# Odd pairs of heads on exchanged halves of the partitions in a retention and feed-forward kernel

## The chip, the cores and the metric

The kernel runs on one core of one Trainium2 chip. The metric is the device time of one execution in microseconds (us), the median of several runs. Engines are named as in the profile: PE is TensorE (PEld its weight loads), DVE is VectorE, ACT is ScalarE, POOL is GpSimd, SP is SyncE, which issues the DMAs (SPq is its queue).

## What is computed

The reference takes q, k and v of 4 batches, 8 heads, 576 positions and 64 values a head, and computes a retention, followed by two feed-forward parts:

```python
scores = scale * np.matmul(q, k.transpose(0, 1, 3, 2))
Dmat = np.where(rel >= 0, gamma[:, None, None] ** rel[None, :, :], 0.0)
ret = scores * Dmat[None, :, :, :]
x = np.matmul(ret, v)            # then (B*S, H*D) = 2304 x 512
a, b = x @ w1, x @ w2            # 512 -> 1024
x = (a * b @ w3) @ w_out         # 1024 -> 1024 -> 512
h = x @ w_in                     # 512 -> 2048
g = np.maximum(h, 0) + alpha * np.minimum(h, 0)
out = g @ w_out                  # 2048 -> 512
```

The change is in the retention alone.

## The kernel before

The retention is computed in chunks of 128 positions (four of 128 and one of 64), with a running state of 64 x 64 per head. Two heads make a pair: head 2p of pair p has its q and k on partitions 0 to 63, head 2p+1 on partitions 64 to 127 (`HEADS`). Four pairs make a batch. All products of the retention are of fp32 operands.

For a chunk c the class `Retention` issues, on PE, in this order within one step (`steps`, L340): `scores(c+1)`, `values(c)`, `moments(c+1)`.

- `scores` (L256) multiplies the keys of a chunk by its queries, for each pair m and each half `pp` of the partitions: 64 rows of the array, 128 columns, into one bank for each half (L274). The last chunk gives 64 x 64 (L264). VectorE multiplies the result by a mask into `rt` (L277; `rte` for the last chunk, L266).
- `moments` (L281) multiplies scaled keys by values: 128 rows, 64 columns of the array, 64 wide (L288). VectorE makes the new state of it (L294, L296, L298), with the decay `gc` of each head.
- `values` (L303) makes the output `o` of a chunk: state times queries (L312: rows `pp`, columns `pp`), then `rt` times v (L320: 128 rows, 64 columns; for the last chunk `rte` times the end of v, rows and columns `pp`). So of the four quarters of the array that a 64 x 64 product can lie in, L312 uses the two on the diagonal. `o` has two buffers of one bank each. VectorE multiplies `o` by `qs` (L327), ScalarE rounds the result to `xh` (L172), VectorE takes the rest as `xl` (L173).

```python
for m, p in enumerate(self.pairs):
    for pp in HEADS:
        nc.tensor.matmul(o[pp, m, 0:w], self.state[c - 1][pp, m], qk[p][pp, 0, i0:i0 + w],
                         start=(m == 0), stop=False, skip_group_check=True)
```

PE, ACT and SP work their instructions in the order in which the program issues them. VectorE's and ScalarE's parts are put into a list (`later`) and issued at the next `flush()`. ScalarE also scales the keys of a batch before its first moments (`prep`, L253).

Batch 0 is computed first, by itself: pairs 0 and 1 (`r0`, `s0`) and pairs 2 and 3 (`r1`, `s1`) are two sequences of steps that are merged by a written-out order (L392), with two pairs in each step. Its loads are issued at the very start by SP: `per_row` (kd and gc, L375), then for each pair qk (L358), kv (L359) and the pair's constants `per_pair` (mask, mtail and qs, L361), with two loads of weights between. Before the first loads land, PE runs 16 products on zeros (L385).

Then the products by w1 and w2 begin (`ab_unit`, `gemm3`, L179), in sets of 12 products of 128 x 512. Batches 1, 2 and 3 are computed with four pairs in a step, and `cycle` (L450) puts their steps between those sets: batch 1 at 7/6 steps a set, so that two steps may follow each other at once (and what is left follows at L472), batch 2 at 7/15, batch 3 at 7/9. The loads of a batch are issued where the one before has freed the tiles: those of batch 1 after the last step of `s0` (L399) and after batch 0 (L406), those of batch 2 at L475, those of batch 3 at L487. A load waits until the load eight before it has landed, as the kernel's program has eight semaphores for loads. After 220 us nothing of the retention is left.

Of the kernel before, what the change touches and what calls it, by code (L numbers as in the profile page):

```python
# [7 lines left out]
F32 = mybir.dt.float32  # L8
# [4 lines left out]
ALU = mybir.AluOpType  # L13
PSUM = bass.MemoryType.PSUM
DRAM = bass.MemoryType.DRAM

P = 128
B, H, S, D = 4, 8, 576, 64
NPAIR = H // 2
NT, DM, DF1, DF2 = B * S, 512, 1024, 2048  # L20
CH = 128
# [4 lines left out]
HEADS = (slice(0, 64), slice(64, 128))  # L26
# [111 lines left out]
def retention_moe_kernel(ctx: ExitStack, tc, qk, kv, w_out1, w3t, w12, w_in, w_out2, alpha, c_row, c_pair, out):  # L138
    nc = tc.nc

    def pool(stack, name, bufs=1, **kw):
        return stack.enter_context(tc.tile_pool(name=name, bufs=bufs, **kw))
# [14 lines left out]
    idle = tmp.tile([P, 512], I32, tag="b", name="idle", bufs=2).bitcast(BF16)  # L157
# [12 lines left out]
    def split(hi, lo, src):  # L170

        nc.scalar.copy(hi, src)  # L172
        nc.vector.tensor_tensor(out=lo, in0=src, in1=_f32(hi), op=ALU.subtract)  # L173
# [51 lines left out]
    per_pair = decay.tile([P, NPAIR, 3 * CH + 64], F32, name="per_pair")  # L225
    mask = per_pair[:, :, 0:2 * CH].rearrange("p n (h i) -> p h n i", h=2)
    mtail = per_pair[:, :, 2 * CH:2 * CH + 64]
    qs = per_pair[:, :, 2 * CH + 64:]
    per_row = decay.tile([P, 128], F32, name="per_row")[:, 0:H + NPAIR]
    kd, gc = per_row[:, 0:H], per_row[:, H:]  # L230
# [3 lines left out]
    def x_block(n):  # L234
        if n not in xt:
            w = BLOCKS[n][1]
            xt[n] = tuple(xp.tile([P, KT, 512], F32R, tag=f"x{m}", name=f"x{m}{n}", bufs=3)[:, :, :w] for m in "hl")
        return xt[n]

    class Retention:  # L240


# [13 lines left out]
        def scores(self, c):  # L256
            b, n = self.b, self.n
            sc = self.psum["sc"].tile([P, 2, 512], F32, tag="sc", name=f"sc{b}_{c}")
            qk, v = qkt[b], kvt[b]
            if c == NCH - 1:  # L260
                rt = self.rt[c] = attn.tile([P, NPAIR, 64], F32, tag="rte", name=f"rte{b}")[:, 0:n]
                for m, p in enumerate(self.pairs):
                    for pp in HEADS:
                        nc.tensor.matmul(sc[pp, 0, m * 64:(m + 1) * 64], qk[p][pp, 1, 512:S], qk[p][pp, 0, 512:S],  # L264
                                         start=True, stop=True, skip_group_check=True)
                later.append(lambda: nc.vector.tensor_tensor(  # L266
                    out=rt, in0=sc[:, 0, 0:64 * n].rearrange("p (n i) -> p n i", n=n), in1=mtail[:, self.ps],
                    op=ALU.mult))
                return
            i0 = c * CH  # L270
            rt = self.rt[c] = attn.tile([P, 2, NPAIR, CH], F32, tag="rt", name=f"rt{b}_{c}", bufs=2)[:, :, 0:n]
            for m, p in enumerate(self.pairs):
                for j, pp in enumerate(HEADS):
                    nc.tensor.matmul(sc[:, j, m * CH:(m + 1) * CH], qk[p][pp, 1, i0:i0 + CH], qk[p][pp, 0, i0:i0 + CH],  # L274
                                     start=True, stop=True, skip_group_check=True)

            later.append(lambda: nc.vector.tensor_tensor(  # L277
                out=rt, in0=sc[:, :, 0:n * CH].rearrange("p h (n i) -> p h n i", n=n), in1=mask[:, :, self.ps],
                op=ALU.mult))

        def moments(self, c):  # L281

            b, n = self.b, self.n
            v = kvt[b]
            st = self.psum["st"].tile([P, NPAIR, D], F32, tag="st", name=f"st{b}_{c}")[:, 0:n]
            for m, p in enumerate(self.pairs):
                for j, pp in enumerate(HEADS):
                    nc.tensor.matmul(st[pp, m], v[p][:, 4 * j + c], v[p][:, 8 + 4 * j + c],  # L288
                                     start=True, stop=True, skip_group_check=True)

            def state():
                new = attn.tile([P, NPAIR, D], F32, tag="S", name=f"S{b}_{c}", bufs=3)[:, 0:n]
                if c == 0:
                    nc.vector.tensor_copy(new, st)  # L294
                else:
                    nc.vector.tensor_tensor(out=new, in0=self.state[c - 1], in1=gc[:, self.ps].unsqueeze(2)  # L296
                                            .to_broadcast([P, n, D]), op=ALU.mult)
                    nc.vector.tensor_tensor(out=new, in0=new, in1=st, op=ALU.add)  # L298
                self.state = {**(self.state or {}), c: new}

            later.append(state)

        def values(self, c):  # L303
            b, n = self.b, self.n
            w = CH if c < NCH - 1 else 64
            i0 = c * CH
            qk, v, rt = qkt[b], kvt[b], self.rt.pop(c)
            o = self.psum["o"].tile([P, NPAIR, CH], F32, tag="o", name=f"o{b}_{c}", bufs=2)
            if c:
                for m, p in enumerate(self.pairs):  # L310
                    for pp in HEADS:
                        nc.tensor.matmul(o[pp, m, 0:w], self.state[c - 1][pp, m], qk[p][pp, 0, i0:i0 + w],  # L312
                                         start=(m == 0), stop=False, skip_group_check=True)
            for m, p in enumerate(self.pairs):
                for j, pp in enumerate(HEADS):
                    if c < NCH - 1:
                        vj, rj = v[p][:, 8 + 4 * j + c], rt[:, j, m]
                    else:
                        vj, rj = v[p][pp, 16], rt[pp, m]
                    nc.tensor.matmul(o[pp, m, 0:w], vj, rj, start=(c == 0 and m == 0), stop=True,  # L320
                                     skip_group_check=True)
            later.append(lambda: self.decayed(c, o, w))

        def decayed(self, c, o, w):

            x = xsp.tile([P, NPAIR, CH], F32, tag="x", name=f"xs{self.b}_{c}")[:, 0:self.n, 0:w]
            nc.vector.tensor_tensor(out=x, in0=o[:, 0:self.n, 0:w], in1=qs[:, self.ps, 0:w], op=ALU.mult)  # L327
            t0 = self.b * S + c * CH
            cuts = [0] + [t - t0 for t, _ in BLOCKS if t0 < t < t0 + w] + [w]

            def parts():
                for lo, up in zip(cuts, cuts[1:]):
                    n = (t0 + lo) // 512
                    at = t0 + lo - BLOCKS[n][0]
                    xh, xl = (m[:, self.ps, at:at + up - lo] for m in x_block(n))
                    split(xh, xl, x[:, :, lo:up])

            later.append(parts)
# [13 lines left out]

    qkt, kvt = {b: {} for b in range(B)}, {b: {} for b in range(B)}

    def load_pair(b, p):
        qkt[b][p] = attn.tile([P, 2, S], F32, tag=f"qk{p}", name=f"qk{b}_{p}")
        kvt[b][p] = attn.tile([P, 17, D], F32, tag=f"kv{p}", name=f"kv{b}_{p}")
        nc.sync.dma_start(out=qkt[b][p], in_=qk[b, p])  # L358
        nc.sync.dma_start(out=kvt[b][p], in_=kv[b, p])  # L359
        if b == 0:  # L360
            nc.sync.dma_start(out=per_pair[:, p], in_=c_pair[:, p])  # L361

    def load_batch(b):
        for p in range(NPAIR):
            load_pair(b, p)

    def attention_psum(stack, twice):
        return {"sc": pool(stack, f"ps_sc{twice}", bufs=twice, space=PSUM, reuse_waits="tile"),
                "st": pool(stack, f"ps_st{twice}", space=PSUM, reuse_waits="tile"),
                "o": pool(stack, f"ps_o{twice}", space=PSUM, reuse_waits="tile")}  # L370


    first = ExitStack()
    psum0 = attention_psum(first, 2)
    nc.sync.dma_start(out=per_row, in_=c_row)  # L375
    load_pair(0, 0)
    ws.load_until(1)
    load_pair(0, 1)
    ws.load_until(2)
    load_pair(0, 2)  # L380
    load_pair(0, 3)
    nc.sync.dma_start(out=al, in_=alpha)
    warm = psum0["o"].tile([P, 512], F32, tag="o", name="warm", bufs=2)
    for _ in range(16):
        nc.tensor.matmul(warm, idle[:, 0:P], idle[:, :512], start=True, stop=True)  # L385
    r0, r1 = Retention(0, [0, 1], psum0), Retention(0, [2, 3], psum0)
    r0.prep([0])
    ws.tick(2)
# [74 lines left out]
    def retention(b):  # L463
        r = Retention(b, list(range(NPAIR)), psum1)
        return Steps([r.prep] + r.steps())

    r = retention(1)
# [20 lines left out]
    r = retention(3)  # L488
# [25 lines left out]
    turn = 0  # L514
# [48 lines left out]
    for k in range(C1):  # L563
        ws.until(n_w12 + 3 * k + 3)
        for i in range(C1):
            if k == 0:
                acc[i] = bank(i, f"pw{i}")
            h, l = w3p[i // 4, k]
# [181 lines left out]
    for b in range(NB):  # L750
        ys = [bank(b % 2 * 4 + o, f"y{b}_{o}")[:, :W] for o in range(KT)]
        for c in range(C1):
            to_load.tick(1)
            for o in range(KT):
                oc = slice(o * P, (o + 1) * P)
                for i, (a, bb) in enumerate(((0, 0), (0, 1), (1, 0))):
                    nc.tensor.matmul(ys[o], wpc[c][a][:, oc], yab[b, c][:, bb], start=(c == 0 and i == 0),  # L757
                                     stop=(c == C1 - 1 and i == 2))
# [211 lines left out]
    for n, (j, b) in enumerate(steps):  # L970
# [8 lines left out]
        h, l = ready.pop(n)  # L979
        for i in range(NM):  # L980
            ic = slice(i * P, (i + 1) * P)
            for m in range(2):
                wh, wl = wbc[2 * j + m]
                for q, (x, y) in enumerate(((h, wh), (h, wl), (l, wh))):
                    nc.tensor.matmul(accs[b][i], x[:, m, ic], y, start=(j == 0 and m == 0 and q == 0),  # L985
                                     stop=(j == C1 - 1 and m == 1 and q == 2))
# [83 lines left out]
```

## Time and profile before

| | us |
|---|---|
| median of 3 runs | 814.14 |
| lowest and highest run | 812.62, 814.38 |
| profiled execution: its own time | 812.48 |
| profiled execution: its span | 810.7 |

The profile is of one execution. Its rows give starts in us from the start of the span; in a timeline the second number is how long it took, in a group of instructions the busy time and the mean of one in ns. [...]

### The profile page before, as it was taken

How to read it: one execution, taken by the hardware profiler on the slowest of the kernel's cores; microseconds unless marked ns; L12 is line 12 of the kernel's file. 1: busy time of each engine (PE TensorE's matmuls, PEld its weight loads, DVE VectorE, ACT ScalarE, POOL GpSimd, SP SyncE). 2: the span in 40 equal slices, each digit the busy share in tenths (PEclk: the TensorE clock that was granted, in tenths of full speed). 3: DMA queues.
4: the chain of work that ended last, by engine and by line, in shares of the span. 5: the costliest groups of instructions: out<-in, count | busy, mean ns of one | idle time of the engine just before them, and what ended most of it. 6: DMA issues, size and time to landing. Idle time of an engine off the chain costs nothing.

```text
span 810.7 us, 12667 instructions
## 1 busy us (share of the span) xinstructions
PE 793.1 (98%) x4768; PEld 699.9 (86%) x4768; DVE 499.6 (62%) x895; ACT 349.7 (43%) x648; POOL 0.2 (0%) x4
## 2 busy tenths in 40 slices
PE   7989999999999999999999999999999999999998
PEld 4768888888888988999999999999997888888886
DVE  4786776325467789979752568677889923222222
ACT  3452562232245566655534455455566622222221
POOL 0000000000000000000000000000000000000000
PEclk8989999999999999999999999999999999999999
DMA  9845821371076658999934935325566735344341
GB/s 348 300 142 200 303 112 78 105 280 79 27 229 181 213 184 300 308 375 402 394 129 151 380 116 186 127 98 186 172 212 223 238 98 175 97 138 137 98 135 40
DMA packets 78845, 155.91 MB, mean 192 GB/s; under 512 B 7872, under 2 KB 55488, under 8 KB 78784
## 3 DMA queue, kind: packets, MB, share of 16 engines
q1 hardware_dynamic: 78784, 155.10, 54.5%
q8 instruction: 37, 0.61, 0.3%
q14 instruction: 24, 0.20, 0.1%
HBM read 103.69 MB, written 51.38 MB: 191 GB/s over the span
## 4 chain that ended last, share of the span: by engine, by line
PE 92%; DMA 3%; ACT 2%; DVE 1%; SPq 1%; issue 0%; ACTq 0%
PE ps L179 24%; PE o L985 23%; PE h L824 21%; PE y L757 12%; PE pw L571 5%; PE o L320 2%; DMA kv<-in_kv_dram 2%; PE sc L274 2%; PE o L312 1%; DMA gr<-gd 1%; PE st L288 1%; DVE xs L327 0%; ACT xh L172 0%; PE sc L264 0%; DVE gl L173 0%
## 5 line engine op out<-in xcount | busy, mean ns | idle before, releaser
L179 PE MATMUL ps<-xh,w 128*128 128x512 f32 (+1 forms) x640 | 187.5, 374 | 1.8 <-ACT w L112 1.7
L985 PE MATMUL o<-wb,gh 128*128 128x512 f32 x576 | 177.6, 389 | 1.2 <-ACT gh L172 1.2
L179 PEld LDWEIGHTS ps<-xh,w 128*128 128x128 f32 x640 | 116.9, 190 | 23.7 <-ACT w L112 1.9
L985 PEld LDWEIGHTS o<-wb,gh 128*128 128x128 f32 x576 | 108.0, 188 | 24.0 <-ACT gh L172 1.7
L179 PE MATMUL ps<-xl,w 128*128 128x512 f32 (+1 forms) x320 | 118.8, 371 | 0.0
L985 PE MATMUL o<-wb,gl 128*128 128x512 f32 x288 | 112.3, 390 | 0.5 <-DVE gl L173 0.5
L173 DVE TENSOR_TENSOR gl<-gr,gh 128x768 fp32r<-128x768 f32 x48 | 45.9, 957 | 100.2 <-ACT gh L172 100.0
L757 PE MATMUL y<-yab,wp 128*128 128x384 f32 x576 | 100.0, 334 | 0.0
L757 PEld LDWEIGHTS y<-yab,wp 128*128 128x128 f32 x576 | 99.9, 188 | 0.1
L172 ACT CAST gh<-gr 128x768 fp32r<-128x768 f32 x48 | 40.2, 839 | 116.2 <-PE o L985 111.3
L179 PEld LDWEIGHTS ps<-xl,w 128*128 128x128 f32 x320 | 60.9, 190 | 10.0 <-DVE xl L173 0.3
L985 PEld LDWEIGHTS o<-wb,gl 128*128 128x128 f32 x288 | 54.0, 188 | 12.4 <-DVE gl L173 1.3
L836 DVE SCALAR_TENSOR_TENSOR g<-m,al,g 128x384 f32<-128x384 f32 x48 | 29.7, 618 | 48.2 <-ACT g L835 47.9
L824 PE MATMUL h<-xT,wv 128*128 128x384 f32 x288 | 54.9, 334 | 1.4 <-DVE g L842 1.4
L824 PE MATMUL h<-xT,wu 128*128 128x384 f32 x288 | 55.0, 335 | 0.3 <-ACT h L849 0.3
L108 DVE CUSTOM_DVE_ANT_0 a<-a,b 128x1024 uint16<-128x1024 uint16 x72 | 49.5, 687 | 3.8 <-DVE a L106 0.5
L824 PEld LDWEIGHTS h<-xT,wv 128*128 128x128 f32 x288 | 50.3, 188 | 1.8 <-DVE g L842 1.8
L824 PEld LDWEIGHTS h<-xT,wu 128*128 128x128 f32 x288 | 50.3, 188 | 0.9 <-ACT h L849 0.6
L433 ACT CAST ab<-f 128x512 fp32r<-128x512 f32 (+1 forms) x40 | 23.1, 576 | 64.2 <-DVE f L437 59.8
L437 DVE TENSOR_TENSOR f<-f,ps 128x512 f32<-128x512 f32 (+1 forms) x40 | 25.3, 632 | 35.3 <-PE ps L179 35.0
L103 DVE TENSOR_SCALAR a<-a 128x512 f32<-128x512 f32 x72 | 30.4, 422 | 22.2 <-ACT a L93 21.9
L571 PE MATMUL pw<-wo,w 128*128 128x512 f32 x192 | 43.7, 389 | 0.0
(82 smaller groups left out, 1012.9 us busy)
## 6 DMA issues: line engine op xcount, KB each, us to landing
gd<-g SPq DMA_DIRECT2D x96, 192.0 KB, 1.9
gr<-gd SPq DMA_DIRECT2D x96, 192.0 KB, 2.5
abd<-ab SPq DMA_DIRECT2D x32, 512.0 KB, 3.7
raw<-in_w_out_dram SPq DMA_DIRECT2D x24, 512.0 KB, 4.0
qk<-in_qk_dram SPq DMA_DIRECT2D x16, 576.0 KB, 7.1
yab<-abd SPq DMA_DIRECT2D x24, 384.0 KB, 8.5
kv<-in_kv_dram SPq DMA_DIRECT2D x16, 544.0 KB, 7.9
raw<-in_w_dram SPq DMA_DIRECT2D x16, 512.0 KB, 7.4
```

The source lines that it names most:

```text
L103: nc.vector.tensor_scalar(out=a, in0=a, scalar1=self.LEAST, scalar2=self.MOST, op0=ALU.max, op1=ALU.min)
L108: nc.vector.tensor_tensor(out=a.bitcast(I32), in0=a.bitcast(I32), in1=b, op=ALU.add)
L172: nc.scalar.copy(hi, src)
L173: nc.vector.tensor_tensor(out=lo, in0=src, in1=_f32(hi), op=ALU.subtract)
L179: nc.tensor.matmul(ps, a, bb, start=(n == 0), stop=(n == last))
L433: nc.scalar.copy(t[:, 0], f)
L437: nc.vector.tensor_tensor(out=f, in0=f, in1=pss[1], op=ALU.mult)
L571: nc.tensor.matmul(acc[i], a[:, ic], bb, start=(k == 0 and n == 0), stop=(k == C1 - 1 and n == 2))
L757: nc.tensor.matmul(ys[o], wpc[c][a][:, oc], yab[b, c][:, bb], start=(c == 0 and i == 0), stop=(c == C1 - 1 and i == 2))
L824: nc.tensor.matmul(ps, a[:, x, ks], b[:, y, k], start=(fresh and n == 0), stop=(n == 5), skip_group_check=True)
L836: nc.vector.scalar_tensor_tensor(out=g, in0=r, scalar=neg[:, c:c + 1], in1=g, op0=ALU.mult, op1=ALU.add)
L985: nc.tensor.matmul(accs[b][i], x[:, m, ic], y, start=(j == 0 and m == 0 and q == 0), stop=(j == C1 - 1 and m == 1 and q == 2))
```

## The change

- A function `places(p)` gives for each of the two heads of pair p: the half of the partitions on which its q, k and state lie, the half on which its output lies, and the number of the former. For even pairs both are the head's own half, as before; for odd pairs q, k and state lie on the other half, and the output stays.
- The scores, moments, state products and the end of v follow it. Both heads' products are issued head by head as before, so in odd pairs the one on partitions 64 to 127 comes first. The output `o` of even pairs and of odd pairs lies in two banks, and successive chunks take turns in different columns of the same two banks (`values_room`), where before each chunk had a bank to itself, one of two. The first product of each bank has `start`.
- L327 reads both banks in one instruction and writes as before.
- The loads of odd pairs are exchanged: qk as two loads of 64 partitions, kv as one load of its first 16 columns of 64 and two half-loads of the end of v; in batch 0 mask as two loads, mtail as two half-loads and qs as one, where each of these pairs had one load of constants. kd and gc, one load before, are four: kd, gc of even pairs, and two halves of gc of odd pairs.

No arithmetic changes. The core of the diff:

```diff
+    def places(p):
+
+        return [(HEADS[(j + p) % 2], HEADS[j], (j + p) % 2) for j in range(2)]
...
-                    for pp in HEADS:
-                        nc.tensor.matmul(sc[pp, 0, m * 64:(m + 1) * 64], qk[p][pp, 1, 512:S], qk[p][pp, 0, 512:S],
+                    for rows, _, _ in places(p):
+                        nc.tensor.matmul(sc[rows, 0, m * 64:(m + 1) * 64], qk[p][rows, 1, 512:S], qk[p][rows, 0, 512:S],
...
-                for j, pp in enumerate(HEADS):
-                    nc.tensor.matmul(sc[:, j, m * CH:(m + 1) * CH], qk[p][pp, 1, i0:i0 + CH], qk[p][pp, 0, i0:i0 + CH],
+                for rows, _, r in places(p):
+                    nc.tensor.matmul(sc[:, r, m * CH:(m + 1) * CH], qk[p][rows, 1, i0:i0 + CH], qk[p][rows, 0, i0:i0 + CH],
...
-                for j, pp in enumerate(HEADS):
-                    nc.tensor.matmul(st[pp, m], v[p][:, 4 * j + c], v[p][:, 8 + 4 * j + c],
+                for j, (rows, _, _) in enumerate(places(p)):
+                    nc.tensor.matmul(st[rows, m], v[p][:, 4 * j + c], v[p][:, 8 + 4 * j + c],
...
-            o = self.psum["o"].tile([P, NPAIR, CH], F32, tag="o", name=f"o{b}_{c}", bufs=2)
+            o = self.psum["o"](n)
             if c:
                 for m, p in enumerate(self.pairs):
-                    for pp in HEADS:
-                        nc.tensor.matmul(o[pp, m, 0:w], self.state[c - 1][pp, m], qk[p][pp, 0, i0:i0 + w],
-                                         start=(m == 0), stop=False, skip_group_check=True)
+                    for rows, pp, _ in places(p):
+                        nc.tensor.matmul(o[pp, p % 2, m // 2, 0:w], self.state[c - 1][rows, m], qk[p][rows, 0, i0:i0 + w],
+                                         start=(m < 2), stop=False, skip_group_check=True)
             for m, p in enumerate(self.pairs):
-                for j, pp in enumerate(HEADS):
+                for j, (rows, pp, r) in enumerate(places(p)):
                     if c < NCH - 1:
-                        vj, rj = v[p][:, 8 + 4 * j + c], rt[:, j, m]
+                        vj, rj = v[p][:, 8 + 4 * j + c], rt[:, r, m]
                     else:
-                        vj, rj = v[p][pp, 16], rt[pp, m]
-                    nc.tensor.matmul(o[pp, m, 0:w], vj, rj, start=(c == 0 and m == 0), stop=True,
+                        vj, rj = v[p][rows, 16], rt[rows, m]
+                    nc.tensor.matmul(o[pp, p % 2, m // 2, 0:w], vj, rj, start=(c == 0 and m < 2), stop=True,
                                      skip_group_check=True)
...
-            nc.vector.tensor_tensor(out=x, in0=o[:, 0:self.n, 0:w], in1=qs[:, self.ps, 0:w], op=ALU.mult)
+            nc.vector.tensor_tensor(out=x.rearrange("p (i r) w -> p i r w", r=2),
+                                    in0=o[:, :, :, 0:w].rearrange("p r i w -> p i r w"),
+                                    in1=qs[:, self.ps, 0:w].rearrange("p (i r) w -> p i r w", r=2), op=ALU.mult)
...
+    def in_places(p, t, src):
+
+        if p % 2 == 0:
+            nc.sync.dma_start(out=t, in_=src)
+        else:
+            for rows, pp, _ in places(p):
+                nc.sync.dma_start(out=t[rows], in_=src[pp])
+
     def load_pair(b, p):
...
-        nc.sync.dma_start(out=qkt[b][p], in_=qk[b, p])
-        nc.sync.dma_start(out=kvt[b][p], in_=kv[b, p])
-        if b == 0:
+        in_places(p, qkt[b][p], qk[b, p])
+        if p % 2:
+            nc.sync.dma_start(out=kvt[b][p][:, 0:16], in_=kv[b, p, :, 0:16])
+            in_places(p, kvt[b][p][:, 16], kv[b, p, :, 16])
+        else:
+            nc.sync.dma_start(out=kvt[b][p], in_=kv[b, p])
+        if b == 0 and p % 2 == 0:
             nc.sync.dma_start(out=per_pair[:, p], in_=c_pair[:, p])
+        elif b == 0:
+            for h in range(2):
+                nc.sync.dma_start(out=per_pair[:, p, h * CH:(h + 1) * CH],
+                                  in_=c_pair[:, p, (1 - h) * CH:(2 - h) * CH])
+            in_places(p, mtail[:, p], c_pair[:, p, 2 * CH:2 * CH + 64])
+            nc.sync.dma_start(out=qs[:, p], in_=c_pair[:, p, 2 * CH + 64:])
...
+    def values_room(stack, twice):
+
+        t = pool(stack, f"ps_o{twice}", space=PSUM, reuse_waits="tile").tile([P, 2, 512], F32, name=f"o{twice}")
+        turn = [0]
+
+        def take(n):
+            at = turn[0] % 512
+            turn[0] += n // 2 * CH
+            return t[:, :, at:at + n // 2 * CH].rearrange("p r (i w) -> p r i w", w=CH)
+
+        return take
...
-    nc.sync.dma_start(out=per_row, in_=c_row)
+    nc.sync.dma_start(out=kd, in_=c_row[:, 0:H])
+    for p in range(2):
+        in_places(p, gc[:, p::2], c_row[:, H + p::2])
...
-    warm = psum0["o"].tile([P, 512], F32, tag="o", name="warm", bufs=2)
-    for _ in range(16):
-        nc.tensor.matmul(warm, idle[:, 0:P], idle[:, :512], start=True, stop=True)
+    warm = psum0["o"](8).rearrange("p r i w -> p r (i w)")
+    for n in range(16):
+        nc.tensor.matmul(warm[:, n % 2], idle[:, 0:P], idle[:, :512], start=True, stop=True)
```

## Rows read from the trace of the kernel before

**Rows 1.** The profile's page: busy us of each engine, its share of the span, instructions.

```profile
PE 793.1 (98%) x4768; PEld 699.9 (86%) x4768; DVE 499.6 (62%) x895; ACT 349.7 (43%) x648; POOL 0.2 (0%) x4
```

**Rows 2.** Chain of waits over the span, longest pieces: start us, us, what.

```profile
4.20 7.35 DMA kv<-in_kv_dram
...
34.14 8.44 DMA kv<-in_kv_dram
45.76 5.02 PE ps L179 x12
...
114.56 1.09 PE sc L274 x16
```

**Rows 3.** Timeline, a step of batch 2: start us, us, engine, line, operation, records.

```profile
131.24 1.09 PE L312 MATMUL o<-qk,S 64*64 64x128 f32 x16
132.26 1.09 PE L320 MATMUL o<-rt,kv 128*64 128x128 f32 x16
...
133.41 0.69 DVE L327 TENSOR_TENSOR xs<-o,per_pair 128x512 f32<-128x512 f32 x1
...
140.55 1.09 PE L312 MATMUL o<-qk,S 64*64 64x128 f32 x16
```

**Rows 4.** PE's timeline in windows 12.13-12.20, 10.68-10.75, 57.53-57.60: records in each.

```profile
12.13 0.27 PE L288 MATMUL st<-kv 128*64 128x64 f32 x1 [1.12 <-ACT kv L253]
...
10.68 0.28 PE L288 MATMUL st<-kv 128*64 128x64 f32 x2
...
57.36 0.44 PE L312 MATMUL o<-qk,S 64*64 64x128 f32 x4
```

**Rows 5.** Timeline, the last two steps of batch 1 (68 to 74 us).

```profile
71.95 0.68 PE L312 MATMUL o<-qk,S 64*64 64x64 f32 x16
72.07 0.69 DVE L327 TENSOR_TENSOR xs<-o,per_pair 128x512 f32<-128x512 f32 x1 [0.46 <-PE o L320]
72.32 0.33 SPq L358 DMA_DIRECT2D qk<-in_qk_dram  x1
...
72.47 0.63 PE L320 MATMUL o<-rte,kv 64*64 64x64 f32 x16
...
73.25 0.50 PE L179 MATMUL ps<-xh,w 128*128 128x512 f32 x1 [0.15 <-ACT xh L172]
```

**Rows 6.** Chain of waits in batch 0, the state products on it.

```profile
16.78 1.05 PE o L312 x8
```

**Rows 7.** Stretches: us, busy by engine (records), PE's clock, DMA share, GB/s.

```profile
7.00:13.00 6.00, 2.16 (x19) 1.34 (x18) 2.93 (x5) 3.03 (x6) 0.00 (x0) 0.96 1.03 419
13.00:19.20 6.20, 6.20 (x56) 5.22 (x56) 5.65 (x14) 2.15 (x4) 0.00 (x0) 0.50 1.03 415
...
28.00:32.40 4.40, 4.00 (x64) 2.94 (x64) 3.48 (x11) 1.11 (x3) 0.00 (x0) 1.00 1.01 407
32.40:34.00 1.60, 1.21 (x13) 0.98 (x12) 1.13 (x5) 0.41 (x1) 0.00 (x0) 1.00 0.74 223
34.00:39.00 5.00, 5.00 (x24) 3.87 (x24) 2.73 (x6) 3.62 (x8) 0.00 (x0) 1.00 0.90 286
```

**Rows 8.** Timeline of SP's queue, issues of loads: start us, us, line.

```profile
0.73 0.39 SPq L375 DMA_DIRECT2D per_row<-const_row_dram  x1
1.17 0.42 SPq L358 DMA_DIRECT2D qk<-in_qk_dram  x1
...
25.62 0.33 SPq L358 DMA_DIRECT2D qk<-in_qk_dram  x1
```

**Rows 9.** Timeline of batch 0: scaling, moments and a tail's neighbours.

```profile
19.70 1.70 ACT L253 ACTIVATE kv<-kv,per_row 128x256 f32<-128x256 f32 x4
...
22.00 0.45 PE L288 MATMUL st<-kv 128*64 128x64 f32 x8
...
25.25 0.45 PE L312 MATMUL o<-qk,S 64*64 64x64 f32 x8
...
25.74 0.41 DVE L327 TENSOR_TENSOR xs<-o,per_pair 128x256 f32<-128x256 f32 x1
```

More of the change, by code (lines that the diff above doesn't have):

```diff
@@ L369, in attention_psum @@
                 "st": pool(stack, f"ps_st{twice}", space=PSUM, reuse_waits="tile"),
-                "o": pool(stack, f"ps_o{twice}", space=PSUM, reuse_waits="tile")}
+                "o": values_room(stack, twice)}
     first = ExitStack()
     psum0 = attention_psum(first, 2)
-    nc.sync.dma_start(out=per_row, in_=c_row)
+    nc.sync.dma_start(out=kd, in_=c_row[:, 0:H])
+    for p in range(2):
+        in_places(p, gc[:, p::2], c_row[:, H + p::2])
     load_pair(0, 0)
```

## The prediction

> **What bounds the kernel now.** I read the busy shares first [rows 1]: TensorE is busy 98% of the span, VectorE 62%, ScalarE 43%, so a gain has to come off TensorE's path, and a new wait anywhere on that path is paid in full. The chain of waits [rows 2] says where this holds. From 45.76 us to the end it is TensorE almost alone. Before that it leaves TensorE twice, both times for a load of keys and values: 7.35 us that land at 11.57 (batch 0, pair 1) and 8.44 us that land at 42.62 (batch 1, pair 3). After the second, ScalarE has to scale the keys before it turns to other work, and TensorE goes on at 45.76. So the change has three stages to be costed: batch 0 (to 33.2 us), the wait for batch 1's loads, and batches 1 to 3 among the large products.
>
> In the last of these, one step of a batch of four pairs is a run of small products [rows 3]: after eight scores (1.09 us, start to start [rows 2]) eight state products take 1.02 (131.24 to 132.26), then come the products with the values. An fp32 product leaves two records, so eight leave 16. I asked how many are under way at once, with very narrow windows [rows 4]. Where only one head's keys were ready (12.13), one record is there in the first 0.07 us; where both heads were ready (10.68), two are. Of the state products, begun at 57.36, four have started by 57.60, two more than the first two: they go in twos, one of each head, and 16 records in 1.02 us make a pair every 0.11 to 0.13, taken as 0.11. Two of the array's corners work, two are idle.
>
> **Part 1: four corners instead of two (gain).** In odd pairs the state and q of a head lie on the other half of the partitions while its output stays, so consecutive pairs use all four corners. If four records go where two went, eight pairs of records become four fours: 4 x 0.11 = 0.44 us off each state group of 1.02. The 64-wide tails (state product and L320 with rte, 0.52 each [rows 5]) go in pairs of about 0.06, so 0.23 off each. Batches 2 and 3 have three wide groups and two tails: 3 x 0.44 + 2 x 0.23 = 1.78 us each, 3.55 together, all on the path, where TensorE is alone [rows 2]. Lower bound 0: no row shows four corners at work.
>
> In batch 1 the tails follow the last wide step at once [rows 5]: L312 begins at 71.95, while VectorE's read of the former output (L327) begins at 72.07 and takes 0.69; the next large product waits for ScalarE, fed by that read. Three wide groups bring 1.31; the tails' gain is hidden by this wait. Moreover both outputs now lie in the same two banks, so I let the tail wait for the read to end, which costs 0.2 more than the gain hides: 1.1 us in all for batch 1. Elsewhere in batches 1 to 3 the read ends long before the next values (134.10 against 140.55 [rows 3]), so sharing the banks costs nothing there. That one half of a bank is guarded against a read of the other is my assumption; below it the price is 0. [...]
>
> In batch 0 a group has two pairs. [...] Two of four pairs fall away each time, the later two at full clock: 0.43 + 0.22 + 0.22 = 0.87. After 23.9 us the chain goes through VectorE and ScalarE, so later savings there count as 0.
>
> **Part 2: order of the other products (0).** Scores and moments of odd pairs now come head 1's half first: A B B A instead of A B A B. Taken one half after the other, each of the three seams in a group of four pairs could cost a slot of 0.11 in scores and 0.06 in moments and tails: 2.2 us a batch, the upper bound. I take 0, the lower: in [rows 4] the second head's first record already starts ahead of the first head's second one, so TensorE passes over work whose corner is busy, and A B B A asks for no more of it.
>
> **Part 3: more and smaller loads (loss).** Issues at the start are 0.44 to 0.47 us apart [rows 8]. kd and gc come as four instead of one: 3 x 0.46 = 1.4 us before the first q and k. Bandwidth is used up from there (419 GB/s and full engines from 7 to 13 us [rows 7]), so everything behind moves by as much.
>
> Pair 1's qk comes as two loads of 64 partitions. The trace has no load of 64 partitions. Whole, its 576 KB take 1.41 us at 419 GB/s. Halved, they take from 1.41 (each half half as long) to 2.82 (each half as long as the whole). I take 2.82: the full stretches move 407 to 419 GB/s whatever they load [rows 7], so I read the limit as one of the path into the partitions, of which a half-load uses half; the lower end would need the other half's path to serve it. Price 1.41 per odd pair. [...]
>
> Pair 1's other added pieces (two for the end of v, two of mask, two of mtail, qs by itself) move the bytes that the whole loads moved. They are issued 0.33 to 0.47 us apart while 1.4 MB is still under way before them, so issuing stays ahead of the transfers: 0 to 0.5, taken as 0, since the queue ran ahead by 7 us before (issue 4.20, landing 11.57). So the landing at 11.57 moves by 1.4 + 1.4 = 2.8. On the way through batch 0: minus 0.87 (part 1). Pair 3's keys come 4.2 later (2.8 and its own 1.41); ScalarE scaled them from 19.70 (behind pair 2's) for moments at 22.00 [rows 9], which TensorE now waits for: 0.6. The first tail of batch 0 (25.25) now waits for a read that begins at 25.74 and takes 0.41 [rows 9]: 0.95. Later reads there are on the VectorE chain already: 0. Shift at the end of pair 0 and 1: 2.8 - 0.87 + 0.6 + 0.95 = 3.5 us. What the lower clock may give back (less work falls into its stretch) or take, I bound by 1.4 either way and take as 0.
>
> Batch 1's eight loads begin there (25.62 [rows 8]) and end at 42.62. Two odd pairs add 2 x 1.41. The dip at 32.4 to 34 (223 GB/s against 407 [rows 7]) came from the second four being issued late, and goes: 0.7; the slower stretch after it (286) may go too: 1.5 more. I take 1.2 back. Shift of the landing, and of 45.76: 3.5 + 2.8 - 1.2 = 5.1 us (from 3.1 to 6.3).
>
> In batches 2 and 3 the added issues and 2.8 us of loading are hidden: batch 2's first load is issued at 72.32 [rows 5], its first product starts at 114.56 [rows 2]. If that cover went, 2.8 would be paid.
>
> **Sum.** -3.55 - 1.1 + 5.1 = +0.45 us against the profiled execution's 812.48 us, which lies 1.7 below the median of the runs, 814.14. Forecast: **814.6 us**, no change that can be told (0.2%, 1.6 us, is about what a measurement of this kernel can tell).
>
> **Rivals.**
> - **Halves cost nothing extra** (1.41 per odd pair falls away). For it: all engines serve either load with packets of the same length. Against it: the reading above. Shift in batch 0: 1.4 - 0.87 + 0.95 = 1.5, without added loading and with 0.9 back: 0.6. Sum -3.55 - 1.1 + 0.6 = -4.0: 810.1 us.
> - **Still two at a time** (slower than before). Place: L312 and L320's tails on TensorE. If the next corner's record starts only when the first corner's second one has, part 1 falls away: 3.55 + 1.1 + 0.87 = 5.5 dearer, 820.1 us; it decides once less than four fifths of that gain comes (1.2 us missing make 815.8, slower by 0.2%). For it: no row has more than two under way. Against it: rows and columns of the array both overlap already [rows 3, 4]. [...]
> - **A B B A stalls**: 2.2 us a batch over three batches, 6.6, to 821.2 us; evidence as in part 2.
> - **The wait for shared banks isn't there**: 0.2 + 0.95 less, 813.5 us; no sign changes.
>
> **How the numbers follow.** Forecast with its bounds 0.60 (814.6, within 811.5 to 817.5); halves for nothing 0.17; two at a time, wholly or in part, 0.18; A B B A 0.05. The range reaches from the first rival's time to near the second's: **810 to 819.5**. Faster by over 0.2%: 0.14 from the first rival and 0.13 from the forecast's lower bounds, 0.27. Slower: 0.21 of the two slower rivals and 0.15 from the forecast's upper bounds, 0.36. Same: 0.37.
>
> **What would show it.** Four records of L312 under way in a window of 0.05 us and groups of 0.6 us instead of 1.02 confirm part 1; groups of 1.02 refute it. Scores still at 1.09 confirm part 2. The landing of batch 0's pair 1 near 14.4 us confirms part 3, near 13 the first rival; TensorE resuming near 50.9 confirms the shift. Idle time of L312 ended by L327 shows the shared banks. If the time from that point to the end is not 4 to 5 us shorter, part 1 is wrong.

## The result and the profile after

The changed kernel took 819.59 us (median of 4 runs, 818.74 to 821.27) beside 813.40 for the kernel before in the same job: ratio 1.0079, 95% interval 1.0061 to 1.0096. That is 6.2 us slower, where no change was forecast, and just outside the range given. The profiled execution took 818.74 us, with a span of 817.0; it is compared below with that of before (812.48 and 810.7), a difference of 6.3.

The busy time of TensorE fell by 3.5 us while the span grew by 6.3, so TensorE waits more. The page of after, against [rows 1]:

```profile
PE 789.6 (97%) x4768; PEld 695.6 (85%) x4768; DVE 498.9 (61%) x895; ACT 349.6 (43%) x648; POOL 0.2 (0%) x4
```

The chain of waits of after (start us, us, what) is to be read against [rows 2]:

```profile
18.30 8.65 DMA kv<-in_kv_dram
26.98 0.92 ACT kv L260 x2
27.89 2.48 issue
...
45.33 6.24 DMA kv<-in_kv_dram
51.57 2.22 issue
...
56.89 5.20 PE ps L179 x12
62.09 1.09 PE sc L281 x16
...
68.71 0.60 PE o L319 x16
...
81.98 0.70 DVE xs L334
82.73 0.46 PE o L319 x16
83.42 41.08 PE ps L179 x180
124.50 1.09 PE sc L281 x16
...
166.20 27.43 PE ps L179 x120
193.63 1.09 PE sc L281 x16
...
224.46 69.50 PE ps L179 x396
```

Before, batch 0's last load on the chain was pair 1's, landing at 11.57. Now it is pair 3's, landing at 26.95, and TensorE resumes among the large products at 56.89 instead of 45.76; this point is called the resumption below. The "issue" at 51.57 is still loading: the keys and values of batch 1's pair 3, issued at 45.33, land 8.4 us later by the load's own record, at 53.72. From the resumption on TensorE is almost alone, as before, and gains. The chain of before has these pieces beside those of [rows 2]:

```profile
50.79 1.09 PE sc L274 x16
...
73.25 41.31 PE ps L179 x180
...
158.09 27.43 PE ps L179 x120
185.52 1.09 PE sc L274 x16
...
218.17 69.50 PE ps L179 x396
```

Cut at these pieces, the two executions and the best of the experiments (e1, below) compare so, in us:

| stage | before | after | e1 |
|---|---|---|---|
| start to the resumption | 45.76 | 56.89 | 44.86 |
| to batch 1's second scores | 5.03 | 5.20 | 5.38 |
| batch 1, to the large products alone | 22.46 | 21.33 | 21.37 |
| to batch 2 | 41.31 | 41.08 | 41.09 |
| batch 2 | 43.53 | 41.70 | 41.70 |
| to batch 3 | 27.43 | 27.43 | 27.43 |
| batch 3 | 32.65 | 30.83 | 30.83 |
| to the end of the span | 592.53 | 592.54 | 592.34 |

Two things happened, and they can be told apart at the resumption: 11.1 us are lost before it, 4.8 are won behind it.

**The gain.** A group of eight state products takes 0.60 us where it took 1.02 [rows 3]. Narrow windows on TensorE's timeline of after (68.75 to 68.80, 68.80 to 68.90) show why: four records have started 0.16 us after the first (by 68.80), eight after 0.26 (by 68.90), where before four had started after 0.24 [rows 4].

```profile
68.64 0.34 PE L319 MATMUL o<-qk,S 64*64 64x128 f32 x4
...
68.64 0.45 PE L319 MATMUL o<-qk,S 64*64 64x128 f32 x8
```

**The loss.** SP's queue in the timeline of after, against [rows 8]: the last large load of pair 1, then weights and pair 2's q and k, then alpha (8 KB, the factor of the second feed-forward part).

```profile
6.79 0.58 SPq L377 DMA_DIRECT2D kv<-in_kv_dram  x1
...
15.33 0.33 SPq L85 DMA_DIRECT2D raw<-in_w_dram  x1
15.71 0.43 SPq L367 DMA_DIRECT2D qk<-in_qk_dram  x1
...
27.04 0.54 SPq L423 DMA_DIRECT2D al<-in_alpha_dram  x1
```

In the timeline of before, pair 2's q and k stand here:

```profile
5.94 0.44 SPq L358 DMA_DIRECT2D qk<-in_qk_dram  x1
```

They were issued at 5.94 before; now at 15.71, when pair 1's big loads had landed (15.32). By then seven small loads behind pair 1's keys hold seven of the eight places, and nothing of size is under way. The stretches of after show it in the last two columns (DMA share, GB/s), where [rows 7] had full engines at 415 to 419:

```profile
7.00:12.80 5.80, 1.26 (x9) 0.52 (x7) 0.57 (x2) 2.12 (x4) 0.00 (x0) 0.80 1.05 316
12.80:14.20 1.40, 0.77 (x2) 0.48 (x2) 1.22 (x3) 0.00 (x0) 0.00 (x0) 0.50 0.92 244
15.70:18.00 2.30, 2.10 (x14) 1.65 (x16) 1.24 (x3) 0.55 (x2) 0.00 (x0) 0.50 0.68 212
```

There are two different losses in it: up to 14.2 the DMA engines are full, or nearly so, and move little (the halves); from 15.7 to 18 they are a third empty (the held queue). A third stands in VectorE's timeline and what surrounds it, to be read against [rows 9]:

```profile
25.34 0.28 DVE L303 TENSOR_TENSOR S<-S,per_row 128x128 f32<-128x128 f32 x1
26.98 0.91 ACT L260 ACTIVATE kv<-kv,per_row 128x256 f32<-128x256 f32 x2 [1.20 <-DMA kv<-in_kv_dram]
28.98 0.18 DVE L844 TENSOR_SCALAR al<-al 128x16 f32<-128x16 f32 x1 [3.35 <-DMA al<-in_alpha_dram]
...
30.00 0.28 DVE L305 TENSOR_TENSOR S<-S,st 128x128 f32<-128x128 f32 x1
...
30.38 0.46 PE L295 MATMUL st<-kv 128*64 128x64 f32 x8 [3.88 <-issue]
```

Pair 3's keys are scaled at 27.89, but the moments start at 30.38. They write the bank that VectorE's L305 reads at 30.00, and L305 stands in VectorE's order behind a small operation on alpha, whose load SP issued last of all. The view says "issue" because the wait is for several things; the last to end, by these rows, is L305 (at 30.28).

Behind that wait stands a fourth loss, in TensorE's clock. From 26.4 to 30.3 us TensorE works 0.10 us; its granted clock is still 1.00 up to 30.9 and then 0.50 up to 34.3. Before, it was 1.00 from 19.5 to 43.2. The same 48 records, from the moments at 30.38 to the end of the stretch at 34.59, against e1 with whole loads (21.67 to 24.38), columns as in [rows 7]:

```profile
30.38:34.59 4.21, 4.21 (x48) 3.26 (x50) 2.85 (x8) 0.54 (x2) 0.00 (x0) 0.59 1.00 403
```

```profile
21.67:24.38 2.71, 2.71 (x48) 2.18 (x50) 2.06 (x7) 0.55 (x2) 0.00 (x0) 1.00 0.94 378
```

So the lower clock takes 1.5 us here. That it fell because TensorE had waited is not shown.

### The profile page after: what moved, and what is told of

It is laid out like the page before. It is cut to its first block, busy times and chain, and to the rows that moved or that the text cites. A ratio compares the mean times of both kernels' runs of the same rounds, so it can differ in the third digit from the quotient of the medians.

```text
span 817.0 us, 12708 instructions
## 1 busy us (share of the span) xinstructions
PE 789.6 (97%) x4768; PEld 695.6 (85%) x4768; DVE 498.9 (61%) x895; ACT 349.6 (43%) x648; POOL 0.2 (0%) x4
## 4 chain that ended last, share of the span: by engine, by line
PE 90%; DMA 5%; DVE 2%; ACT 1%; SPq 1%; issue 1%; ACTq 0%; DVEq 0%
PE ps L179 24%; PE o L1026 22%; PE h L865 21%; PE y L798 12%; PE pw L612 5%; DMA kv<-in_kv_dram 3%; PE o L327 2%; PE sc L281 2%; DMA qk<-in_qk_dram 1%; PE o L319 1%; PE st L295 1%; DMA gr<-gd 1%; SPq L370 0%; DVE gl L173 0%; DMA x2d<-ys 0%
## 5 line engine op out<-in xcount | busy, mean ns | idle before, releaser
L179 PE MATMUL ps<-xh,w 128*128 128x512 f32 (+1 forms) x640 | 187.6, 375 | 1.7 <-ACT w L112 1.7
L179 PEld LDWEIGHTS ps<-xh,w 128*128 128x128 f32 x640 | 117.2, 190 | 23.3 <-ACT w L112 1.8
L179 PE MATMUL ps<-xl,w 128*128 128x512 f32 (+1 forms) x320 | 118.9, 372 | 0.0
L179 PEld LDWEIGHTS ps<-xl,w 128*128 128x128 f32 x320 | 61.0, 191 | 9.7
L103 DVE TENSOR_SCALAR a<-a 128x512 f32<-128x512 f32 x72 | 30.4, 422 | 25.8 <-ACT a L93 25.5
```

The lines of the kernel that those rows point to most:

```text
L103: nc.vector.tensor_scalar(out=a, in0=a, scalar1=self.LEAST, scalar2=self.MOST, op0=ALU.max, op1=ALU.min)
L179: nc.tensor.matmul(ps, a, bb, start=(n == 0), stop=(n == last))
```

## The experiments

Each is an edit of the changed kernel unless another is named. "Resumes" is the first product of L179 after batch 1's loads, as in the table. A time without an interval or a number of runs is of one execution. Executions of one kernel differ by 3 to 5 us (ten of e12: 812.87 to 816.17, ten of e11: 810.25 to 815.27), so these experiments are read by the landings and the resumption in the trace more than by the time. In e2, e5, e6 and e8, moreover, the part behind the retention takes 594.5 to 595.3 us, where all other executions have 592.2 to 592.9: there the granted clock fell to 0.50 once more, between 619 and 640 us. Their times are some 2 us longer in that part, far behind the loads at the start; that the lower clock makes this difference was not tried.

**e1: every load whole.** The order of the halves is put into the layout of the inputs and constants, which the program makes before the launch in any case.

```diff
-            for rows, pp, _ in places(p):
-                nc.sync.dma_start(out=t[rows], in_=src[pp])
...
+        nc.sync.dma_start(out=qkt[b][p], in_=qk[b, p])
+        nc.sync.dma_start(out=kvt[b][p], in_=kv[b, p])
+        if b == 0:
+            nc.sync.dma_start(out=per_pair[:, p], in_=c_pair[:, p])
```

> The changed kernel with the inputs and constants of odd pairs laid out in exchanged halves beforehand, so that every load is whole, as many and as large as in the kernel before; products, order and banks are those of the changed kernel. Theory (the loads' pieces made the loss): TensorE resumes among the large products at 46 to 47 us instead of 56.89, and the stretch from there to the end keeps its gain of 4.8, so the profiled execution takes 808 to 809.5 us. Rival (the waits for the shared banks in batch 0 made it): the resumption stays near 50 and the time at 812 or more.

Measured: 808.41 us (5 runs), ratio to before 0.9948, interval 0.9931 to 0.9965. The chain of e1:

```profile
44.86 5.38 PE ps L179 x12
...
56.90 0.60 PE o L319 x16
...
212.66 69.50 PE ps L179 x396
```

It resumes over 1 us earlier than expected and keeps the gain; the profiled execution took 806.84, 1.2 below the expected range. So the products, their order and their banks cost nothing that can be seen, and the loads made all of the loss. This version is faster than both kernels, by 0.5% against the one before.

**e2 and e3: the loads alone, the banks alone,** both edits of the kernel before.

```diff
+            for rows in HEADS:
+                nc.sync.dma_start(out=t[rows], in_=src[rows])
```

> The kernel before with the loads cut into the same pieces, in the same order, as in the changed kernel, but each half on its own place: no exchange, no shared banks, two corners. Theory (pieces): TensorE resumes at 55 to 57 us instead of 45.76 and the time is 821.5 to 823.5 us, dearer than the changed kernel by the four corners' gain. Rival (shared banks carry some 4 us of it): resumption at 51 to 53, 818 to 819.5 us.

```diff
-            o = self.psum["o"].tile([P, NPAIR, CH], F32, tag="o", name=f"o{b}_{c}", bufs=2)
+            o = self.psum["o"](n)
...
-                        nc.tensor.matmul(o[pp, m, 0:w], self.state[c - 1][pp, m], qk[p][pp, 0, i0:i0 + w],
+                        nc.tensor.matmul(o[pp, m % 2, m // 2, 0:w], self.state[c - 1][pp, m], qk[p][pp, 0, i0:i0 + w],
```

> The kernel before with the values of even and odd pairs in two banks that both buffers share, and nothing else: halves, order and loads as before. Theory (pieces made the loss): batch 0 is dearer by at most 1.5 us, L312 stays at 1.02 us a group since the same two corners work, and the time is 812.5 to 814 us. Rival (shared banks): TensorE resumes 4 us later, 816 to 817 us.

Measured: e2 827.02 us, e3 813.08 (before: 812.89, 8 runs). TensorE's timeline of e2, where it resumes:

```profile
56.68 0.79 PE L179 MATMUL ps<-xh,w 128*128 128x512 f32 x1 [1.66 <-ACT w L112]
```

TensorE's timeline of e3 in batch 0, then the chain of waits of e3:

```profile
19.23 0.65 PE L312 MATMUL o<-qk,S 64*64 64x128 f32 x8 [0.75 <-DVE xs L327]
```

```profile
45.30 5.29 PE ps L179 x12
...
57.21 1.02 PE o L312 x16
```

e2 resumes at 56.68 without any exchange: the loads alone move it by 10.9 of the 11.1 us. (Its time is 3.5 above the expected range; 1.2 us stand right behind the resumption, where it waits for weights once more, and 2.4 us far behind the retention, from 230 us on, as said above.) In e3 L312 does wait for the read of the former output (0.75 in the row), and its groups stay at 1.02: banks alone bring no four corners. Of their waits 0.56 us are left at batch 1's first load (issued at 26.18 instead of 25.62) and nothing at the resumption.

**e5, e6 and e8: which loads.** e5 has only q and k of odd pairs in halves, e6 only the small loads, e8 is e1 with q and k of odd pairs in two loads of all 128 partitions.

```diff
+        # e5
+        in_places(p, qkt[b][p], qk[b, p])
+        nc.sync.dma_start(out=kvt[b][p], in_=kv[b, p])
...
+        # e6
+        nc.sync.dma_start(out=qkt[b][p], in_=qk[b, p])
...
+        # e8
+            for m in range(2):
+                nc.sync.dma_start(out=qkt[b][p][:, m], in_=qk[b, p, :, m])
```

> The changed kernel with only q and k of odd pairs loaded in two halves; the ends of v and the constants are laid out exchanged beforehand and loaded whole, so an odd pair adds one load instead of seven. Theory (the number of small loads made most of the excess): pair 1's keys land near 13, pair 3's near 22.5 us, TensorE resumes at 48.5 to 50, and the profiled execution takes 810.5 to 812.5 us. Rival (two halves at half the rate made it): pair 3's keys land past 25 and TensorE resumes at 53 or later, 815 us or more.

> The reverse: the changed kernel with q and k of odd pairs laid out exchanged beforehand and loaded whole, and with all its small loads (four for the factors, two halves for the end of v, two for the masks, two for the end's mask, one for the scale). The bytes are those of the kernel before. Theory (number of loads): pair 3's keys land at 23 to 25 us, TensorE resumes at 50 to 53, 812.5 to 816 us. Rival (only halves cost): resumption at 46.5 to 47.5, the 1.9 us that the start has more, 809 to 810 us.

> The kernel of e1_whole_loads (everything whole) with q and k of odd pairs in two loads of all 128 partitions, first q, then k: as many loads and as many bytes each as in e5_qk_halves, but over all partitions. Theory (a load of half the partitions holds the DMA engines longer, whatever its number): no stretch of 7 to 12.8 us falls to e5's 261 GB/s, pair 3's keys land at 19.3 to 20.2, TensorE resumes at 44.5 to 46.5 and the time is 806.5 to 809 us. Rival (one load more is what costs): keys past 22, resumption past 49, 812 us or more.

Measured, with the landing of pair 3's keys as the trace has it (e1: 19.31, after: 26.95):

| | time | pair 3's keys | resumes |
|---|---|---|---|
| e8, two whole loads | 809.75 | 19.44 | 45.00 |
| e5, halves | 815.73 | 23.85 | 52.16 |
| e6, small loads | 814.69 | 23.66 | 50.85 |

Stretches of e5, of e6 and of e8, columns as in [rows 7]:

```profile
7.00:12.80 5.80, 0.72 (x7) 0.34 (x3) 1.72 (x4) 1.98 (x4) 0.00 (x0) 0.91 1.02 261
15.70:18.00 2.30, 2.30 (x26) 1.96 (x24) 1.92 (x5) 1.58 (x3) 0.00 (x0) 0.50 1.09 419
```

```profile
7.00:12.80 5.80, 1.99 (x12) 1.02 (x10) 1.32 (x3) 2.13 (x4) 0.00 (x0) 0.81 1.01 393
12.80:14.20 1.40, 0.82 (x8) 0.58 (x6) 0.92 (x2) 0.84 (x2) 0.00 (x0) 0.50 0.42 113
```

```profile
7.00:12.80 5.80, 1.85 (x17) 1.25 (x16) 2.83 (x5) 3.03 (x6) 0.00 (x0) 0.95 1.03 412
```

The two losses are of different kinds. In e5 the DMA engines are full (1.02) and move 261 GB/s; with the same number of loads over all partitions (e8) they move 412. So it is the half of the partitions, not one load more (e8's time lies 0.75 above its range, its landing and its resumption within theirs). In e6 they move 393 as long as there is work and then stand more than half empty (0.42, 113 GB/s): this is the held queue, and e6 came out as expected. My theory for e5 fell: I had expected the halves to be the smaller part, and they cost 4.54 us at pair 3's keys, about as much as the small loads (4.35, of which 1.8 is the later start: pair 0's q and k land at 7.42 instead of 5.61). The landing and the resumption of e5 lie between those of the theory and of the rival. The size of the halves' part is known less well than its sign: with the same halves and few small loads the keys land at 22.94, 23.14 and 23.39 in e10, e11 and e12 (below), 3.6 to 4.1 us behind e1.

**e7 and e9: the small loads from another queue.** e9 is e7 with alpha first.

```diff
-    def in_places(p, t, src):
+    def in_places(p, t, src, queue=nc.gpsimd):
...
+    # e9
+    nc.gpsimd.dma_start(out=al, in_=alpha)
```

> The changed kernel with the small loads (factors, ends of v, constants of odd pairs) issued by GpSimd, which has no other work, instead of SP; the halves of q and k stay with SP. Theory (SP's queue is held because an issue waits for an earlier load to land, and small loads use these places up): if the places are counted by queue, SP issues pair 2's q and k near 7 us instead of 15.71, pair 3's keys land at 22 to 24.5 and the time is 811 to 814 us. If the places are shared by the queues, or the bytes in halves set the pace, pair 2's q and k are still issued past 14 us and the time is within 1.5 us of the changed kernel's 818.7.

> The kernel of e7_other_queue (small loads issued by GpSimd) with alpha's load issued first on GpSimd's queue. In e7 pair 2's q and k were issued at 6.17 and pair 3's keys landed at 24.53, but VectorE waited for alpha (landed 24.70) with the decays of pairs 0 and 1 behind it. Theory (the held queue and alpha's load are two links of one chain): TensorE resumes at 49.5 to 52.5 instead of 58.52, 811.5 to 815 us. Rival (alpha is only named, the halves set all of it): over 817 us.

Measured: 820.66 and 819.78 us; the first product of L179 stands at 56.64 and 55.50 (after: 56.89), and in both a second wait of 0.7 us for weights ends at 58.52 and 57.38. SP's queue in the timeline of e7:

```profile
6.17 0.44 SPq L367 DMA_DIRECT2D qk<-in_qk_dram  x1
```

VectorE's waits in e7 from 5 to 30 us (us in total, times, longest):

```profile
DVE al L844 <- DMA al<-in_alpha_dram: 3.9, 1, 3.9
```

The queue is free (pair 2's q and k at 6.17 instead of 15.71, pair 3's keys land at 24.53, 2.4 earlier), as expected, and yet nothing is won: alpha, landing at 24.70, now holds VectorE for 3.9 us, with the next masks and decays behind it. In e9 alpha is early and another load takes its place. From e9's VectorE timeline:

```profile
17.84 0.43 DVE L103 TENSOR_SCALAR a<-a 128x512 f32<-128x512 f32 x1 [0.42 <-ACT a L93]
...
20.57 1.28 DVE L284 TENSOR_TENSOR rt<-sc,per_pair 128x512 f32<-128x512 f32 x2
```

The second piece of weights lands at 17.11 (13.34 in e1), and the preparation of weights (L103 to L116) stands in VectorE's order ahead of the masks of pairs 0 and 1 (L284). In both runs the granted clock is 0.50 up to 29.9 and 29.2 us, where before it was 1.00 from 19.5 on; how much of the time this takes was not tried. With the halves still in place, the theory that the queue and alpha are the whole chain fell.

**e4, e10, e12 and e11: alpha.** One edit, in three surroundings: e4 of the changed kernel, e10 of e5, e11 of e12, which has only its constants laid out exchanged (q, k and v untouched).

```diff
     load_pair(0, 1)
+    nc.sync.dma_start(out=al, in_=alpha)
     ws.load_until(2)
     load_pair(0, 2)
     load_pair(0, 3)
-    nc.sync.dma_start(out=al, in_=alpha)
```

> The changed kernel with the load of alpha issued right behind pair 1's instead of behind pair 3's. In the changed kernel VectorE waits 3.35 us for it (to 28.98) with batch 0's decay and state behind it. Theory (this wait is one of the links): the wait goes, moments of pair 3 start at about 28.3 instead of 30.34, TensorE resumes 1.5 to 2.5 us earlier, 816 to 817.3 us. Rival (pair 3's keys, landed at 26.95, set the time anyway): under 0.5 us, 818.2 to 819 us.

> The kernel of e5_qk_halves with alpha's load issued behind pair 1's loads. There pair 3's keys landed at 23.85, alpha at 24.57, and pair 3's moments began at 26.19. Theory (alpha's wait on VectorE is a link): moments begin within 1.2 us of the keys' landing instead of 2.34, TensorE resumes 0.8 to 1.5 us earlier than 52.16, 814 to 815 us. Rival: no difference within 0.4 us.

> The changed kernel with only its constants laid out exchanged beforehand and loaded whole (the arrays q, k and v as before, so q and k of odd pairs and the end of v still come in halves); alpha's load last, as in the changed kernel. Theory: near e5_qk_halves, which lacks only the halves of v's end: pair 3's keys at 23.5 to 25, TensorE resumes at 52 to 53.5, 815 to 817 us.

> The kernel of e12_constants_only with alpha's load issued behind pair 1's loads, the one difference between the two. Theory (alpha's wait on VectorE is a link, which e10 showed at 2.9 us at the resumption and e4 did not show, since there pair 3's keys happened to land 1.5 us later): 2.5 to 4 us less than e12, that is 811.5 to 814 us, no slower than the kernel before. Rival (e4 is the rule, e10 an accident of the loads): within 1 us of e12, 814.5 us or more.

| surroundings | alpha last | alpha early | resumes |
|---|---|---|---|
| all pieces: after, e4 | 818.74 | 818.16 | 56.89, 56.80 |
| halves: e5, e10 | 815.73 | 811.75 | 52.16, 49.27 |
| halves, v's ends: e12, e11 | 814.19 | 812.41 | 52.73, 49.22 |

The first two rows compare single executions, the third medians of 10 runs: ratio to before 1.0026 (1.0010 to 1.0041) for e12 and 0.9998 (0.9980 to 1.0016) for e11. VectorE's row of e12, and the chain of e11 where TensorE resumes:

```profile
24.20 0.17 DVE L836 TENSOR_SCALAR al<-al 128x16 f32<-128x16 f32 x1 [1.83 <-DMA al<-in_alpha_dram]
```

```profile
49.22 4.79 PE ps L179 x12
```

The wait is a link: without it pair 3's moments begin 2.9 us earlier in e10 (23.33 instead of 26.19) and 2.1 us earlier in e11 (23.54 instead of 25.60), and TensorE resumes 2.9 and 3.5 us earlier in the profiled executions. Not all of this is the wait. In e10 pair 3's keys also land 0.9 us earlier than in e5; and e5 and e12 have a stretch at a granted clock of 0.50 (25.4 to 32.2 and 31.6 to 35.0 us) where e10 and e11 have 1.00. Whether alpha's wait brings that stretch was not tried. The medians of e12 and e11 lie 1.8 us apart, with intervals that just overlap. That is less than the 2.5 to 4 I expected and more than the rival's 1; executions of one kernel differ here by 3 to 5 us (e12: 812.87 to 816.17). (e12's median lies 0.8 below its range, its resumption within.) In e4 the theory fell: the wait went too, but pair 3's keys landed at 28.45 instead of 26.95, and TensorE's granted clock was 0.50 from 24.8 to 33.5 us. Why they landed later there was not settled by a run.

## Why the prediction was wrong

**Part 1 (four corners) held.** Forecast 1.78 us for batches 2 and 3 each and 1.1 for batch 1; measured 43.53 - 41.70 = 1.83, 32.65 - 30.83 = 1.82, and 22.46 - 21.33 = 1.13. The price of 0.11 us for a pair of records was read from [rows 3, 4] and carried over unchanged. What it brought in batch 0 (0.87 in the sum) can't be read off in after, as that stage is set by the loads. The first term of the 0.87 takes a pair of records at a granted clock of 0.50 as twice 0.11 us, which no run shows by itself. In its place: in e1's chain the first group takes 0.63 us (16.73, granted clock 0.50 from 15.7 to 18), 0.42 less than before [rows 6, 7], and the second 0.38 (19.70), where the chain of before has 0.58 (20.02).

**Part 2 (order A B B A, 0) held.** Scores still take 1.09 us a group; the lower bound was the right end.

**Shared banks:** the waits are there (TensorE waits 3.7 us for L334 up to 43 us in after, and batch 1's last state products, at 82.73, follow its read at 81.98 as forecast), but e3 is the same as before within its measurement. 0.95 in batch 0 was too much: 0.56 in e3, and nothing at the resumption.

**Part 3 (loads) failed, and with it the forecast.** Predicted shift of the resumption 5.1 us (bounds 3.1 to 6.3), measured 11.1. Up to the end of pairs 0 and 1, where batch 1's loads begin, I had 3.5, and it was 35.66 - 25.62 = 10.0. The sign set for this part was off from the start: batch 0's pair 1 landed at 15.32, where 14.4 was to confirm it. The stretch behind batch 0 was right (1.6 against 1.1). From batch 1's first issue to its last landing it is 17.0 us before, 15.6 in e1 and 18.1 in after: against e1 the pieces cost 2.4 us, where I had 2.8, and with whole loads 1.3 came back, where I had 1.2. By its terms, at the landing of pair 3's keys, where I had 4.2 and the trace has 26.95 - 19.39 = 7.6:

- Halves: I took 1.41 us for an odd pair, the whole load's time once more. Two pairs cost 4.54 in e5, so 2.27 each (1.8 to 2.0 in e10 to e12; in batch 1 only 1.2, ends of v included). The first step that failed is that a load at half rate costs only its own time. The load next to it slows as well: in e5 the first weights take 2.78 us from the landing before theirs, in e1 1.23. That a half-load uses half of one path into the partitions was my reading of [rows 7]; no run shows such a path. What the runs show is the rate: 261 GB/s with full engines in e5's stretch, in which other loads are mixed, against 412 in e8's.
- Small loads: "taken as 0, since the queue ran ahead by 7 us" is the second step that failed. The queue ran ahead because its eight places held large loads; that an issue waits for the load eight before it was left out of this step. With small ones in them the bytes under way run out. They cost 4.35 us in e6, where I had 1.4 for the start and nothing for the rest. Both kinds together cost 7.64 (after against e1), less than their sum; why was not tried.
- Alpha was not in the sum at all. It is issued behind all other loads of batch 0, so every added issue delays it, and its use stands in VectorE's order before batch 0 is done. Before, it was hidden (landing at 20.12, VectorE at 20.37); now VectorE waits 3.35 us for it, up to 28.98.
- "TensorE now waits for: 0.6" at pair 3's keys was worked out from too small a delay, and from the keys alone. The moments at 22.00 [rows 9] moved to 30.38.
- The lower clock was "taken as 0", with 1.4 either way. The stretch at 0.50 behind the moments took 1.5.

**The rivals.** "Still two at a time" gave 820.1 and "A B B A stalls" 821.2, near the time measured, and both are refuted: groups of 0.60, scores of 1.09. "Halves cost nothing" is refuted by e5 and e8. The case that came true, loads dearer than my bound, was inside none of them: I had bounded each load's own transfer and given the queue 0 to 0.5.

## What to carry to other kernels

Where the start of a kernel is bound by loads, count loads and not only bytes: with a fixed number of them under way (eight here), each small one takes the place of a large one (in e6 pair 3's keys land 4.35 us later, 1.8 of it from the later start), and whatever is issued last is delayed by all. Follow that last load to the engine that works in order behind it (alpha and VectorE here, a wait of 3.35 us). Where the program lays out its inputs in any case, an exchange of partitions that is wanted in a product belongs in that layout, which cost nothing here, and not in loads of half the partitions (e1 against after: 12.0 us at the resumption).

## What the runs showed of the hardware

A load of half the partitions slows its neighbours: in e5's stretch the engines were full at 261 GB/s instead of 412 in e8's, although the two halves were only 590 of the 1,514 thousand bytes that it moved (128 x 4,608 bytes; 261 x 5.8). Near the end of that stretch almost only the whole load of keys and values behind the halves is left (48 of the 50 packets of data that begin from 11 to 12 us are its 4,352-byte ones), and it too runs at about half the rate: 218 GB/s against 414 in e1's stretch from 7 to 12.8 us. Its packets take 293 ns at the median, in e1 168:

```profile
11.00:12.00 1.00, 0.48 (x2) 0.29 (x2) 0.93 (x3) 0.40 (x1) 0.00 (x0) 0.86 0.96 218
```

TensorE started two records of a later group 0.05 us ahead of the last two of the former one. From after's timeline:

```profile
80.20 0.33 PE L319 MATMUL o<-qk,S 64*64 64x128 f32 x2
80.25 0.23 PE L271 MATMUL sc<-qk 64*64 64x64 f32 x2
```

The last two records of the scores (L271, issued first) start 0.05 us behind the first two of the state products that follow them. The order A B B A leaves two corners free for pair 1's state products at that point, so these are probably the two; the records do not name the corner. So TensorE's records do not all start in the order in which the products are issued. It fits that A B B A costs nothing (scores 1.09 us as before).
